# Shifted value tiles made on TensorE, global values fetched in one step, and a newly searched instruction order

## The chip, the cores and the metric

The kernel runs on one core of a Trainium2 chip. The metric is the device time of one execution in microseconds (us). Each time comes with the span between the core's first and last instruction, about 2 us shorter, and with the mean clock that was granted to TensorE (1.00 is full speed). That mean needs care: time for which a trace holds no clock record counts as full speed. The first clock record of the kernel before is at 41.88 us, so a 1.00 earlier than that is no measurement. A run counts as fast when it lies within 1.5% of the fastest run of the same kernel, otherwise as slow, and only fast runs are compared. The five jobs of this study ran on five different chips; the number of the chip of the first comparison is not known, and it is called the first chip. One and the same kernel takes up to 5% longer on one chip than on another (the kernel before took 230.06 and 230.41 us on chips 3 and 2, and 238.42 to 241.22 us in the four other comparisons), so a kernel is always compared with the kernel before in the same job.

## The reference

Four sequences of 768 tokens pass through block-sparse attention (8 heads of 64, blocks of 32 tokens), and the result, with its heads joined, passes through a gated MLP block.

```python
# attention: a query block sees its neighbours, the first and last block,
# and 3 sampled blocks; the first and last query block see everything
mask = np.abs(blk_i - blk_j) <= 1
mask = mask | (blk_i == 0) | (blk_j == 0) | (blk_i == n_blocks - 1) | (blk_j == n_blocks - 1)
for qb in range(n_blocks):
    for kb in sampled_blocks[qb]:
        mask[qb*32:(qb+1)*32, kb*32:(kb+1)*32] = True
...                                    # softmax, then attn @ v
# MLP
h = gelu(x @ w_in); u, v = h[..., :512], h[..., 512:]
v_n = layernorm(v) * g_ln
v_s = np.einsum('ts,bsd->btd', w_sg, v_n) + b_sg[None, :, None]
return x + (u * v_s) @ w_out
```

## The kernel before

The kernel names every operation ("pvR0.2" is the product of probabilities and values over the sampled blocks, batch 0, third tile of 128 tokens). One list, SEQ, fixes the order in which the operations are put on the engines. The semaphore waits are worked out from that order. Each engine is given its operations as one list in that order, so an operation that waits holds up those behind it.

```python
SEQ = """
ldk0.3 ident0 csk0.3:A ident1 warm22:0 ...        # some 1,300 names, :A is the engine, :4 the PSUM bank
"""
```

V of a batch is written to a scratch area in DRAM ("sc") and read back in the layouts that the products need: VG (first and last block), VA (tiles at 0, 128, ...), VS (tiles shifted by 64 tokens) and VR (the sampled blocks, gathered by "ga").

```python
for n in range(2):
    def vg_(e, n=n):
        return e.dma_start(vj[64 * n:64 * n + 64, 0, :, :]..., bass.AP(sc.tensor, sc.offset, ...))
    op("SP", f"vg{b}.{n}", vg_, r=[("scr", bp)], w=[("vjg", n)] + ..., dsem=f"vg{n}", nbytes=66560)
...
op("SP", f"vs{b}", lambda e: e.dma_start(VS[:, :, :, :]..., sc[64:704, :]...), r=[("scr", bp)], w=["VS"], nbytes=665600)
```

The product with the gathered values consists of many short matrix products.

```python
def pvr(pe):
    for h in range(H):
        for ib in range(nbk):
            ins = mm(pe, oap(h, 32 * ib, 32), PR[pr_][0:96, c:c + 32], vslot(rgs[ib])[0:96, h, :])
    return ins
op("PE", f"pvR{b}.{tau}", pvr, r=[okey, ("PR", pr_)] + [("VR", rg) for rg in rgs], mode="32", ...)
```

The softmax here doesn't subtract the row's maximum and nothing guards it: scores larger than these inputs give would overflow.

## Time and profile before

| | before |
|---|---|
| time, median of 3 runs | 241.32 us (240.14 to 242.85) |
| profiled span, TensorE clock | 240.6 us, 0.984 |
| TensorE busy, idle | 206.9 us, 33.7 us |
| "issue" waits of TensorE | 5.9 us, 12 times, at most 0.9 (two of them, 0.7 us, before transposes) |
| DMA moved | 41.51 MB |

TensorE bounds the kernel. What can be saved is its idle time, and most of that lies in the first 37 us. An "issue" wait is a stretch in which TensorE waits for nothing that the profile shows. The views themselves are in the prediction.

### The profile page before, as it was taken

What the parts mean: (1) busy time and instruction counts of PE and PEld (TensorE: products, weight loads), DVE (VectorE), ACT (ScalarE), POOL (GpSimd) and SP (SyncE); (2) the same over time, 40 slices, a digit from 0 to 9 for tenths busy, and PEclk for the clock granted to TensorE, in tenths of its full rate; (3) what the DMA queues carried; (4) which work ended last, traced back from release to release, by engine and by line L of the source; (5) the groups of instructions that cost most, each with busy time, mean ns of one, the idle gap of its engine ahead of it and who ended that gap; (6) DMA issues with size and microseconds to landing.
All of it is one profiled execution on the core that took longest, in us unless ns stands there. A gap on an engine that the chain in (4) does not pass through costs nothing.

```text
span 240.6 us, 8125 instructions
## 1 busy us (share of the span) xinstructions
PE 206.9 (86%) x3282; PEld 164.1 (68%) x3282; DVE 157.0 (65%) x469; ACT 166.9 (69%) x254; POOL 109.3 (45%) x207
## 2 busy tenths in 40 slices
PE   5064538879999989999699999799999999999994
PEld 2053426558887678887488687678886778789672
DVE  2453323645796978894648967648668957577694
ACT  3497926868698946898479666578999677976100
POOL 8215984544384856911547373803472752012000
PEclk9999999988999999999979999999999999999999
DMA  6999999759997795985977975690588123311007
GB/s 191 341 368 282 268 198 228 141 116 235 277 212 178 217 241 75 214 130 183 219 192 169 275 150 185 153 179 9 138 258 208 36 54 119 111 46 44 3 0 262
DMA packets 34457, 41.51 MB, mean 173 GB/s; under 512 B 4804, under 2 KB 27620, under 8 KB 34420
## 3 DMA queue, kind: packets, MB, share of 16 engines
q0 software_dynamic: 14208, 16.20, 35.7%
q1 hardware_dynamic: 20212, 24.80, 34.0%
q8 instruction: 26, 0.43, 0.7%
q14 instruction: 11, 0.09, 0.1%
HBM read 39.72 MB, written 9.55 MB: 205 GB/s over the span
## 4 chain that ended last, share of the span: by engine, by line
PE 78%; ACT 9%; DMA 3%; SPq 3%; issue 3%; another core or an unknown queue 2%; DVE 1%
PE PS L335 68%; PE PS L848 5%; PE PS L521 4%; DMA x_tok<-in_q_dram 3%; ACT PW L707 2%; SPq L480 2%; ACT PR L750 1%; ACT QD L331 1%; ACT PG L724 1%; PE PS L659 1%; ACT w_sgT L331 1%; ACT qn L331 1%; ACT L724 1%; ACT bsg L331 1%
## 5 line engine op out<-in xcount | busy, mean ns | idle before, releaser
L616 POOL DMA_INDIRECT VR<-scr,IDX x44 | 43.2, 982 | 20.5 <-issue 8.3
L637 POOL COPY KR<-KT 128x128 bf16 x88 | 26.0, 328 | 24.7 <-PE PS L335 19.9
L335 PE MATMUL PS<-w_sgT,vh 128*128 128x384 bf16 x192 | 33.5, 326 | 0.0
L633 DVE COPY KR<-KT 128x128 bf16 x176 | 28.3, 226 | 4.1 <-PE PS L335 3.2
L335 PE MATMUL PS<-w_in,xg 128*128 128x512 f32 x96 | 28.3, 422 | 3.1 <-ACT xg L331 2.2
L335 PE MATMUL PS<-w_out,xg 128*128 128x512 f32 x96 | 26.3, 409 | 0.0
L335 PE MATMUL PS<-xg,w_in 128*128 128x384 f32 x128 | 26.2, 351 | 0.0
L916 DVE SCALAR_TENSOR_TENSOR gt<-PS,gcol,bsg 128x384 f32<-128x384 f32 x32 | 19.3, 613 | 10.1 <-PE PS L335 9.3
L335 PEld LDWEIGHTS PS<-w_sgT,vh 128*128 128x128 bf16 x192 | 17.9, 98 | 11.0 <-issue 0.4
L750 ACT ACTIVATE PR<-PS 96x1024 bf16<-96x1024 f32 (+1 forms) x23 | 21.7, 962 | 5.0 <-PE PS L335 2.8
L335 PEld LDWEIGHTS PS<-xg,w_in 128*128 128x128 f32 x128 | 23.1, 194 | 1.7 <-ACT QD L331 0.3
L707 ACT ACTIVATE PW<-PS,b_odd 128x512 bf16<-128x512 f32 (+1 forms) x24 | 15.5, 652 | 9.2 <-PE PS L335 9.2
L335 PEld LDWEIGHTS PS<-w_in,xg 128*128 128x128 f32 x96 | 17.2, 194 | 6.9 <-ACT xg L331 2.7
L874 POOL TENSOR_TENSOR lnt<-lnmv,lnc 128x2 f32<-128x2 f32 x12 | 2.4, 200 | 42.5 <-DVE lnmv L870 41.8
L707 ACT ACTIVATE PW<-PS,b_even 128x512 bf16<-128x512 f32 (+1 forms) x24 | 15.6, 651 | 8.0 <-remote 4.4
L934 DVE TENSOR_TENSOR x_tok<-PS,x_tok 128x512 f32<-128x512 f32 x24 | 16.3, 685 | 5.7 <-PE PS L335 5.5
L869 DVE BATCH_NORM_STATS2 lnst<-vg 128x6 f32<-128x512 f32 x24 | 16.1, 682 | 5.6 <-ACT vg L867 5.6
L829 DVE RECIPROCAL rden<-PS 128x8 f32<-128x8 f32 x24 | 4.9, 205 | 22.7 <-PE PS L335 20.6
L335 PEld LDWEIGHTS PS<-w_out,xg 128*128 128x128 f32 x96 | 17.1, 189 | 3.3
L331 ACT ACTIVATE QD<-PS 64x768 bf16<-64x768 bf16 x18 | 14.4, 803 | 6.3 <-PE PS L335 4.5
L724 ACT ACTIVATE PG<-PS 128x512 bf16<-128x512 f32 x24 | 13.9, 598 | 6.4 <-PE PS L335 6.3
L335 PE MATMUL PS<-VA,PW 128*64 128x65 bf16 x384 | 17.5, 199 | 0.1
(122 smaller groups left out, 438.4 us busy)
## 6 DMA issues: line engine op xcount, KB each, us to landing
out_dram<-x_tok SPq DMA_DIRECT2D x20, 256.0 KB, 2.3
VR<-scr SPq DMA_DIRECT2D x114, 32.5 KB
scr<-vj SPq DMA_DIRECT2D x4, 780.0 KB, 4.7
VS<-scr SPq DMA_DIRECT2D x4, 650.0 KB
kn<-in_v_dram POOLq DMA_DIRECT2D x6, 384.0 KB
kn<-in_k_dram POOLq DMA_DIRECT2D x6, 384.0 KB
qn<-in_q_dram POOLq DMA_DIRECT2D x6, 384.0 KB, 7.3
VA<-scr SPq DMA_DIRECT2D x4, 520.0 KB
```

The lines of the kernel that those rows point to most:

```text
L331: return x.activation(o_, i_, ACT.Copy)
L335: return pe.matmul(o, l, r, start=start, stop=True, skip_group_check=True)
L616: return g.indirect_dma_start(out=vt[0:96, :, :].rearrange("p h e -> p (h e)"), out_offset=None, in_=scr[bp][:, :], in_offset=bass.Indirec ...
L633: ins = x.tensor_copy(KR[:, :, rg, 32 * j:32 * j + 32], KT[:, :, bass.ds(vals["DVE", j, i], 32)])
L637: op("POOL", f"kp{b}.{i}", lambda x, i=i, rg=rg: x.tensor_copy(KR[:, :, rg, 64:96], KT[:, :, bass.ds(vals["POOL", 2, i], 32)]), r=kk + [(" ...
L707: return a.activation(o, i_, ACT.Exp, bias=bias[:, 0:1], scale=SCALE)
L724: op("ACT", f"exG{b}.{tau}", aft=ga, fn=lambda a: a.activation(PG[pg_][:, :], PS[:, uG.slot * 512:uG.slot * 512 + 512], ACT.Exp, scale=SCALE),
L750: return a.activation(PR[pr_][0:96, 0:n], PS[0:96, uR.slot * 512:uR.slot * 512 + n], ACT.Exp, scale=SCALE)
L848: ins = pe.transpose(PS[:, cc:cc + P], x_tok[bp][:, tau, kt * P:kt * P + P], ident_f[:, :])
L869: op("DVE", f"bs{b}.{tau}", lambda x: x.bn_stats(lnst[:, vr, :], vg[vr][:, :]), r=[("vg", vr)], w=[("lnst", vr)], dur=0.6, prio=pr - 300)
L916: op("DVE", f"g1{b}.{c}{dt}", lambda x: x.scalar_tensor_tensor(gt[gr][:, :], PS[:, u.slot * 512:u.slot * 512 + 384], gcol[:, dt:dt + 1], b ...
L934: op("DVE", f"res{b}.{tau}", lambda x: x.tensor_tensor(x_tok[bp][:, tau, :], PS[:, u.slot * 512:u.slot * 512 + 512], x_tok[bp][:, tau, :], ...
```

## The change

The intent was to bring V of batch 0 to the products earlier. The shifted tiles no longer make a DMA trip: TensorE multiplies two neighbouring VA tiles with a shifted identity I3. The two transfers of the global values are issued together and counted as one. Last, the whole order was searched again with measured delays, so that nearly all of SEQ differs. A fourth, small part is in the code that works out the waits: an operation of GpSimd right behind a clear or a padding (names that begin with "ze" or "pa") now waits for it. The core of the diff:

```diff
+    op(("DVE", "POOL"), "i3z", lambda x: x.memset(I3, 0.0), w=["I3"], dur=0.2, prio=-200)
+    op("POOL", "i3", lambda g: g.affine_select(I3, I3, ..., base=64, ...), r=["I3"], w=["I3"], ...)
...
-        for n in range(2):
-            def vg_(e, n=n):
-                return e.dma_start(vj[64 * n:64 * n + 64, 0, :, :]...)
-            op("SP", f"vg{b}.{n}", vg_, ..., dsem=f"vg{n}", nbytes=66560)
+        def vg_(e):
+            return [e.dma_start(vj[64 * n:64 * n + 64, 0, :, :]...) for n in range(2)]
+        op("SP", f"vg{b}.0", vg_, ..., dsem="vg0", nbytes=133120, nd=2)
...
+        if b == 0:
+            for t in range(5):
+                def shf(pe, t=t, u=u):
+                    for c in range(2):
+                        for n in range(2):
+                            ins = mm(pe, PS[:, o:o + 260], I3[:, 128 - 128 * c:256 - 128 * c],
+                                     VA[:, t + c, 4 * n:4 * n + 4, :]..., c == 0)
+            ...                                   # and five evictions she0..4 to VS
+        else:
+            op("SP", f"vs{b}", ...)               # batches 1 to 3 as before
...
-ldk0.3 ident0 csk0.3:A ident1 warm22:0 warm3:N warm10:N warm21:N lnc zeva:P ...
+ident0 ident1 warm19:N bias0 bias1 ldk0.0 lnc i3z:P padk csk0.0:A padv ones iota i3 sbi ...
...                                               # all of SEQ
```

## The prediction

> **What bounds the kernel now.** I read the page first, then the busy table cut into stages, then the waits of TensorE, then the first 45 us of the timeline, and last the chain. The page:
>
> ```profile
> PE 206.9 (86%) x3282; PEld 164.1 (68%) x3282; DVE 157.0 (65%) x469; ACT 166.9 (69%) x254; POOL 109.3 (45%) x207
> ...
> PE   5064538879999989999699999799999999999994
> ...
> ACT  3497926868698946898479666578999677976100
> ...
> DMA  6999999759997795985977975690588123311007
> ```
>
> Each digit is a tenth of busy time in a slice of 6 us. TensorE is nearly full from the eighth slice on, and much emptier before. The idle total is 240.6 - 206.9 = 33.7 us; the question is where it lies. The stage table (stretch; its length; busy time and instruction count of TensorE, weight loads, VectorE, ScalarE, GpSimd; clock; DMA share; GB/s) splits it:
>
> ```profile
> 0.00:22.70 22.70, 8.88 (x55) 5.59 (x55) 8.46 (x33) 14.91 (x22) 9.47 (x24) 1.00 0.90 296
> 22.70:37.20 14.50, 7.09 (x204) 5.59 (x205) 4.75 (x24) 8.90 (x15) 12.94 (x28) 1.00 1.09 235
> 37.20:44.00 6.80, 6.55 (x116) 5.17 (x115) 3.53 (x18) 4.55 (x8) 3.10 (x7) 1.00 0.98 212
> 44.00:60.00 16.00, 13.60 (x344) 10.68 (x343) 8.68 (x24) 11.98 (x16) 7.16 (x12) 0.89 0.79 163
> 60.00:108.00 48.00, 46.55 (x766) 38.07 (x764) 38.72 (x115) 37.65 (x57) 28.24 (x49) 1.00 0.93 194
> 108.00:120.00 12.00, 9.17 (x206) 7.35 (x206) 6.97 (x13) 7.94 (x13) 4.29 (x6) 1.00 0.73 198
> ...
> 145.00:160.00 15.00, 13.29 (x298) 10.53 (x297) 10.30 (x37) 9.64 (x15) 7.80 (x15) 1.00 0.78 185
> ```
>
> Length less TensorE busy: 13.8 us idle up to 22.7 (the loads), 7.4 us to 37.2 (first attention steps), 0.3 to 44, 2.4 to 60, 1.5 to 108, 2.8 to 120, 1.7 between 145 and 160, and 3.2 after 235. These make 33.1; the three stretches not shown hold 0.6. So there are three regimes: a head limited by DMA and then by a wait for V, a long middle limited by TensorE, and an end that no order can shorten much.
>
> What holds the head can be read from TensorE's waits:
>
> ```profile
> PE PS L335 <- DVE VG L332: 2.9, 1, 2.9
> PE PS L335 <- ACT w_sgT L331: 2.6, 1, 2.6
> ```
>
> and from the timeline (start, duration, engine, line, operation, idle time before it and what ended it):
>
> ```profile
> 15.53 0.36 SPq L561 DMA_DIRECT2D scr<-vj  x1
> ...
> 20.27 0.69 SPq L572 DMA_DIRECT2D vj<-scr  x1
> ...
> 21.91 0.52 SPq L582 DMA_DIRECT2D VS<-scr  x1
> ...
> 24.90 0.56 SPq L572 DMA_DIRECT2D vj<-scr  x1
> ...
> 32.13 0.56 DVE L332 COPY VG<-vj 64x260 bf16<-64x260 bf16 x2 [3.49 <-DMA vj<-scr]
> 32.84 0.59 PE L335 MATMUL PS<-VG,PG 128*128 128x130 bf16 x4 [2.90 <-DVE VG L332]
> ```
>
> V of batch 0 is written to a scratch area in DRAM (issued at 15.53, landed by 20.27) and read back in several layouts. The second half of the global values is issued only at 24.90, behind VA, VS and a gather, and its data is usable at 32.13, 7.2 us after issue. The first P x V product starts then. ScalarE, which has already filled the four PW buffers, sits idle from 31.52 to 35.88, and the next score product starts at 37.28.
>
> [...]between 22.7 and 37.2 the share is 1.09, with SyncE and GpSimd transfers in flight together, so a transfer removed or postponed there helps its neighbours. [...]I counted the exp/gelu switches of the old and new ScalarE order, 14 and 14.
>
> **The change part by part.**
>
> *Shifted tiles.* VS of batch 0 no longer comes from DRAM. Removed: one transfer of 650 KB out of a congested stretch; at the 235 GB/s moved there, 665600 / 235000 = 2.8 us of DMA time. Added on TensorE: 5 tiles x 4 matmuls of 260 columns[...]. Added on VectorE: 5 evictions of 128x520 floats; the 128x512 eviction to xg takes 679 ns on it, so about 5 x 0.69 = 3.4 us. Both engines are under half busy from 22.7 to 37.2 (7.09 and 4.75 of 14.5), so most lies beside waiting. Two small I3 set-up instructions go to GpSimd.
>
> *Global values in one step.* Both halves are now issued together, straight after the large VA transfer and ahead of all gathers. With scratch landing near the old 20-22 us, issue comes near 22-23 and landing, at the 4-5 us that a transfer needs in this crowd, at 26-28 instead of 32. Two waits become one in each batch; for batches 1 to 3 I count nothing, since no TensorE wait there names this transfer.
>
> *New order, head.* V is asked for earlier in the load list (transfers 2, 3, 6, 7 of 12). That does not bring scratch forward by much: the loads are 4.7 MB, and DMA moved 190, 340 and 363 GB/s in the stretches to 6, 12 and 16 us, 4.6 MB together, so they fill it until about 16.3 us whatever their order, and the new order also starts both V loads of batch 1 (1.5 MB read) at about 14-16 us, where the old one had only 1 MB of w_in at 16.64. The first scores wait for the last Q eviction on ScalarE. The eighth load was usable at 13.58 before; from there the new ScalarE order has seven casts and evictions of about 0.81 us (5.7), the global keys (1.25), the last Q eviction (0.81) and a copy (0.31): 13.6 + 8.1 = 21.7, against 22.77.
>
> Walking on with durations of this timeline: VA landed by about 26; first shift and eviction to 27.5; five VectorE instructions of 0.4 to 0.7 us until the tile that pvW0.0 needs, about 29.5; first P x V at about 30 against 32.84. Up to the first MLP product (mV0.0) the new order then lists 13 groups of TensorE of 0.5 to 1.1 us each, about 9 us with two of the shifts, hence 40.4 if dense. The old one starts mV0.0 at 42.09, but with one 0.66 us transpose group (xT0.1) less done. **Head gain: 1.7 + 0.7 = 2.4 us, rounded to 2.5**, with the shifts' cost already inside.
>
> *New order, middle.* From 44 to 220 TensorE's idle time is about 9 us. Some 3 us of that are short "issue" gaps that I do not expect order to remove. Of the other 6 (xg 2.2, single waits of 0.5 to 0.9, the Q evictions near 75 and 118) a search with better delays may recover a third to a half, and will add some waits of its own. I take **2 us**.[...]
>
> *End.* Same counts of products, of g1, g2 and residual adds; the order differs in detail. **0 to 0.5 us.**
>
> Sum: 2.5 + 2 + 0.3 = 4.8 us; 241.3 - 4.8 = 236.5. I shade this to **236.3**, since the walk assumes no benefit at all from the 2.8 us of DMA time set free.
>
> **Rivals.**
>
> 1. *The early V loads of batch 1 eat the gain.* They share the 16 engines with the last Q loads and with the scratch write. If shared evenly, scratch lands at about 23 instead of 20.3, and the first P x V at 32 or later. For: DMA share is already 0.90 to 1.09 through the head. Against: a search fed with measured landing delays should have seen it. Time: 239 to 241.
> 2. *The new order removes nearly all V waiting, and TensorE stays dense from 28 us.* The 7.4 us before 37.2 fall to about 2 and the middle gives 4. For: ScalarE is idle 4.4 us in the head only for lack of PW buffers. Against: ScalarE itself is busy 8.73 us of the 10 from 20 to 30. Time: about 232.
> 3. *The saved time is given back in the middle*: batch 1's gathers and loads come no earlier, so an earlier TensorE waits for them. For: DMA share stays 0.93 from 60 to 108. Against: after 44 no TensorE wait names a DMA. Time: about 239.
>
> **Range and chances.** The main estimate lies just at the 2% line (236.5). Rivals 1 and 3 sit above it, rival 2 below, and the middle is uncertain by about 2 us either way. Range 231.5 to 240.5. Faster by over 2%: 0.50; within 2%: 0.45; slower by over 2%: 0.05, since only a disturbed middle of more than 7 us could do that.
>
> **What would show it.** Right: global values copied before 28.5 us; first P x V at 29-31; no ScalarE idle time of 4 us in the head; TensorE idle from 22.7 to 37.2 down from 7.4 to about 4-5;[...] busy time of TensorE about 209 us; the idle time from 44 to 220 near 7 us. Wrong: first scores later than 23 us or scratch read back later than 22 (rival 1); first P x V early but mV0.0 no earlier than 42 (head gain lost to ScalarE or to gathers); a new DMA wait of TensorE after 44 (rival 3).

## The result, and the profile after

| | before | changed |
|---|---|---|
| time, median of 4 runs | 241.22 us | 249.06 us (247.18 to 254.18, the last one slow) |
| profiled span, clock | 240.6 us, 0.984 | 247.3 us, 0.965 |
| TensorE busy, idle | 206.9, 33.7 | 213.2, 34.1 |
| "issue" waits | 5.9 us, 12 times | 11.0 us, 22 times |

The ratio is 1.029, with a 95% interval of 1.020 to 1.039. A ratio here is the mean time of one kernel's fast runs over the mean of the other's of the same rounds, so it is not quite the ratio of the medians. The change made the kernel slower by about 3%.

The page of the changed kernel (busy time; busy tenths of TensorE, its clock and the DMA share in 40 slices of 6.2 us):

```profile
PE 213.2 (86%) x3305; PEld 168.7 (68%) x3305; DVE 160.5 (65%) x474; ACT 166.0 (67%) x253; POOL 112.9 (46%) x210
...
PE   1085577758999998899999989899999797999996
...
PEclk9999999965799999999999999999999998899999
DMA  5999989785793977975999994852056535100107
```

TensorE's idle time is what it was, but its busy time has grown by 6.3 us, and the clock has a dip in the ninth to eleventh slice. The stage table, with the columns of the one in the prediction:

```profile
0.00:22.70 22.70, 8.09 (x60) 6.16 (x60) 11.80 (x40) 14.56 (x22) 13.31 (x33) 1.00 0.96 284
22.70:37.20 14.50, 10.54 (x206) 6.78 (x205) 4.91 (x18) 7.77 (x13) 6.96 (x14) 1.00 1.12 221
37.20:44.00 6.80, 5.50 (x130) 3.99 (x129) 3.99 (x14) 4.36 (x7) 4.02 (x10) 1.00 1.00 211
44.00:60.00 16.00, 10.84 (x254) 7.87 (x255) 4.56 (x25) 10.16 (x13) 8.36 (x14) 0.73 0.77 159
60.00:108.00 48.00, 45.62 (x722) 36.90 (x723) 34.05 (x101) 33.14 (x55) 26.56 (x41) 0.95 0.89 190
```

From 22.7 to 37.2 us the idle time fell from 7.4 to 4.0 us, as hoped, but mainly because the shifts themselves fill 3.1 us of that stretch. From 44 to 60 us it rose from 2.4 to 5.2 us, and the clock there fell from 0.89 to 0.73. The first spatial product of the MLP (mS0) started at 83.3 us instead of 77.3, so 6.0 of the 6.7 us of span are lost by then.

How V came in the head (timeline; start, duration, engine, line, operation, and in brackets the idle time before and what ended it):

```profile
13.60 0.36 SPq L568 DMA_DIRECT2D scr<-vj  x1
14.15 0.97 POOL L507 DMA_DIRECT2D kn<-in_v_dram  x1 [0.47 <-POOL iop L448]
...
20.41 1.27 SPq L578 DMA_DIRECT2D vj<-scr  x2
...
21.73 0.45 SPq L586 DMA_DIRECT2D VA<-scr  x1
...
30.63 0.47 DVE L335 COPY VG<-vj 64x260 bf16<-64x260 bf16 x2 [5.16 <-DMA vj<-scr]
...
31.61 1.04 PE L338 MATMUL PS<-VA,bsg 128*128 128x260 bf16 x4 [2.67 <-DMA VA<-scr]
...
34.43 0.62 PE L338 MATMUL PS<-VG,PG 128*128 128x130 bf16 x4
```

The two halves of the global values are indeed issued together at 20.41, but 10 us pass until they are copied. The first tile of VA, issued at 21.73, comes as late: the shift that needs it ("VA,bsg"; I3 lies in the storage of bsg) waited for it in TensorE's queue until 31.61. A load of batch 1's V (`kn<-in_v_dram`) went out at 14.15, between the scratch write and its read. The first product of probabilities and values starts at 34.43, later than the 32.84 of before.

The long stall lies after 47 us, in the product pvR0.2 (timeline of TensorE alone, other instructions left out):

```profile
47.29 0.31 PE L338 MATMUL PS<-VR,PR 96*32 96x65 bf16 x14
...
48.72 0.19 PE L338 MATMUL PS<-VR,PR 96*32 96x65 bf16 x1 [0.53 <-issue]
...
51.60 0.26 PE L338 MATMUL PS<-VR,PR 96*32 96x65 bf16 x3 [1.20 <-issue]
...
53.02 0.33 PE L338 MATMUL PS<-VR,PR 96*32 96x65 bf16 x7 [0.49 <-issue]
```

These 32 products need about 0.45 us together where nothing disturbs them. Here they took 6 us. They advanced by one to three products and then stood still for about 0.7 us, again and again. They are one operation, which waits for its operands only before its first product, so the operands had been there since 47.29. After it the clock was granted at half speed: from 52 to 66 us the mean was 0.53, against 0.88 before.

The stretch at half clock lay from 51.4 to 65.0 us (mean 0.50) and began 3.8 us after the first of these steps. TensorE was not wholly idle in the steps: it was busy for 2.2 of the 6.3 us from 47.0 to 53.3. That the steps brought on the half clock is my inference from the order in time; no run tests it alone.

The groups of TensorE's instructions by shape show how much of the loss lies in these products (busy time and mean of one; idle time before them). First the kernel before, then the changed one:

```profile
L335 PE MATMUL PS<-VR,PR 96*32 96x65 bf16 x656 | 11.2, 201 | 3.2 <-issue 3.2
```

```profile
L338 PE MATMUL PS<-VR,PR 96*32 96x65 bf16 x656 | 13.1, 204 | 6.7 <-issue 6.7
```

The same 656 products took 14.4 us before and 19.8 after, 5.4 us more.

### The profile page after: what moved, and what is told of

It reads as the page before. It is cut to its first block, busy times and chain, and to the rows that moved or that the text cites.

```text
span 247.3 us, 8185 instructions
## 1 busy us (share of the span) xinstructions
PE 213.2 (86%) x3305; PEld 168.7 (68%) x3305; DVE 160.5 (65%) x474; ACT 166.0 (67%) x253; POOL 112.9 (46%) x210
## 4 chain that ended last, share of the span: by engine, by line
PE 80%; DMA 10%; issue 5%; SPq 2%; DVE 2%; ACT 1%; DVEq 0%
PE PS L338 69%; PE PS L879 5%; DMA vj<-scr 4%; PE PS L528 3%; DMA uT<-in_v_dram 3%; DMA scr<-vj 3%; SPq L487 1%; PE PS L690 1%; DVE VS L335 1%; PE PS L1027 1%; ACT PW L805 0%; ACT vj L334 0%; DVE x_tok L965 0%; SPq L578 0%; DVE gt L947 0%
## 5 line engine op out<-in xcount | busy, mean ns | idle before, releaser
L647 POOL DMA_INDIRECT VR<-scr,IDX x44 | 42.7, 971 | 10.9 <-issue 9.5
L338 PE MATMUL PS<-w_sgT,vh 128*128 128x384 bf16 x192 | 34.4, 326 | 0.0
L664 DVE COPY KR<-KT 128x128 bf16 x176 | 27.1, 220 | 1.1 <-ACT KT L334 0.4
L338 PE MATMUL PS<-w_out,xg 128*128 128x512 f32 x96 | 26.9, 413 | 0.0
L338 PE MATMUL PS<-w_in,xg 128*128 128x512 f32 x96 | 26.4, 408 | 0.0
L338 PE MATMUL PS<-xg,w_in 128*128 128x384 f32 x128 | 24.9, 341 | 0.0
L338 PE MATMUL PS<-VA,PW 128*64 128x65 bf16 x384 | 19.1, 203 | 1.2 <-issue 1.2
L338 PEld LDWEIGHTS PS<-w_out,xg 128*128 128x128 f32 x96 | 17.8, 195 | 3.2
L338 PE MATMUL PS<-VR,PR 96*32 96x65 bf16 x656 | 13.1, 204 | 6.7 <-issue 6.7
L338 PEld LDWEIGHTS PS<-VA,PW 128*64 128x64 bf16 x384 | 15.7, 117 | 3.9 <-issue 2.6
```

Source lines behind the costliest of these rows:

```text
L338: return pe.matmul(o, l, r, start=start, stop=True, skip_group_check=True)
L647: return g.indirect_dma_start(out=vt[0:96, :, :].rearrange("p h e -> p (h e)"), out_offset=None, in_=scr[bp][:, :], in_offset=bass.Indirec ...
L664: ins = x.tensor_copy(KR[:, :, rg, 32 * j:32 * j + 32], KT[:, :, bass.ds(vals["DVE", j, i], 32)])
```

## The experiments

With only the two traces at hand my first theory was that batch 1's scratch write, which the new order issues at 46.05 us just before pvR0.2 instead of at 53.60, fills the DMA engines (their busy share was 0.91 from 47.0 to 53.3 us) and so holds up TensorE's short products. The rivals were the early V loads of batch 1, and the order as such. Two notes on what follows: the profiles of e1, e2, e7 and e9 come from runs that count as slow, so what is read from them is weaker; and the verdicts on record of e0, e6, e7, e9, e11, e15 and e18 are "unclear" (for all but e11 the interval reaches below the limit of 1.02), though all these intervals lie above 1.00.

### First job (chip 3; before: 230.06 us)

**e1_late_scratch** and **e2_late_loads** take the suspected traffic away from the short products.

```diff
+    byname["sc1"].deps.append(byname["mV0.2"])        # e1 and e2
-  ... ldk1.0 ... ldq1.0 ...                            # e2: these two behind kp0.22
```

> The changed kernel with one wait added: the scratch write of batch 1's V waits for the MLP product mV0.2, so it no longer runs beside pvR0.2. Theory S (TensorE's short products starve at 0.7 us steps while that write fills the DMA engines, 47.3 to 53.3 us[...]): the stall shrinks from about 5.5 us to under 2, the half-clock stretch from 13.6 us to under 6, and the time falls from 249 to 240-244 us. Rival O (the loss is in the new order's own dependences and in the shifts' added work): stall and clock stay about as they are or the time stays at 246-250 us.

> As the run with the late scratch write, and two loads of batch 1 (half of K, half of Q) issued only after the last gathers of batch 0. Theory S: if these loads also take part in the stall, a further 0 to 2 us less than the run before it (239-243 us), with no stall over 1 us between 44 and 62 us. Rival O: no gain over the late scratch write alone, or a loss of 1-3 us from K of batch 1 coming late.

Measured: e1 239.4 us in the median, but only one of four runs was fast (235.27 us). e2 took 238.79 us, ratio 1.034 (1.026 to 1.041). In e1 pvR0.2 ran undisturbed (0.45 us), and yet its one fast run took 5.2 us more than the kernel before: "issue" waits came to 5.9 us in all, TensorE waited 4.4 us for VA and 2.9 us for QD. That spoke against the scratch write as the whole cause, but the changed kernel itself had not run on this chip, which turned out to matter.

**e3_before_early_scratch** is the mirror: the kernel before, with its scratch write pulled forward.

```diff
-  ... vc1.0 ...                     # where it was
+  ... vc1.0 rec0.2 ...              # so that sc1 can leave earlier, at 47.80 us
```

> The mirror, in the kernel before: only the VectorE copy that releases the scratch write of batch 1 is moved ahead (before the reciprocal of step 2), so that the write is issued near 48-50 us instead of 53.6, into the short products. Theory S: TensorE's unexplained waits between 46 and 60 us grow from 1.4 to 4 us or more, the clock is low for longer than 3.3 us, and the time rises from 241 to 244-249 us. Rival O: within 1 us of 241, for the copy costs VectorE the same wherever it stands.

Measured: 232.56 us, ratio 1.008 (0.999 to 1.017), "issue" waits of 2.4 us. An early scratch write does not do it alone on this chip. As no kernel stalled in steps on this chip, e3 says nothing for the others.

**e5_old_order** keeps the two new parts and goes back to the order of before.

```diff
-SEQ = (the new order)
+SEQ = (the order before, without vg.1 and vs0, with shf0-4, she0-4, i3z, i3 put in,
+       va0.5 behind padv, exW0.21 and exW0.20 earlier)
```

> The first two parts of the change alone: the order of the kernel before, with batch 0's shifted tiles by TensorE and the global values as one step. Theory S: the two parts are nearly neutral or help a little, first P x V near 29-31 us instead of 32.84, time 238-242 us. Rival O (the added work on TensorE and VectorE is the loss): 244 us or more.

Measured: 231.27 us, ratio 1.004 (0.998 to 1.010). With the old order, and on this chip, the shifted tiles and the single step together cost nothing and gain nothing. Here the loss must sit in the order.

### Second job (chip 15; before: 239.23 us)

**e0_changed** is the changed kernel again. **e6_late_v1** moves the two V loads of batch 1 behind w_in0. **e7_old_head** has the old order up to about 80 us and the new one after it. **e8_new_head** is the opposite. Both mixed kernels allocate PSUM banks anew where the two orders disagree.

```diff
-  sc0 ldv1.0 ... ldv1.1 ... w_in0 ... vc1.1 she3 ... she4
+  sc0 ... w_in0 ldv1.0 ldv1.1 ... she3 ... she4 vc1.1         # e6
+SEQ = old[:"qkR1.5"] + (what is left, in the new order)       # e7
+SEQ = new[:"qkQ1.2"] + (what is left, in the old order)       # e8
```

> The changed kernel itself again, because the chip of the first four runs was some 5% faster than the one of the record (230 against 241 us for the kernel before) and the changed kernel was not measured on it. Both theories: ratio to the kernel before 1.02 to 1.045. If the ratio is near 1.00 the whole loss depended on the chip.

> The changed kernel with batch 1's two V loads moved behind w_in in GpSimd's queue, so that they do not share the DMA engines with the last Q loads and the V scratch of batch 0 (and the VectorE copy that takes them moved after the last shifted tile). Theory V (these loads delay the read-back of V, the first shift product waits for VA at the head of TensorE's queue, and everything behind it is late): wait of TensorE for VA from 3-4 us to under 1, first P x V near 29-31 us instead of 33-34, and 2 to 4 us less than the changed kernel. Rival (the loss is elsewhere in the order, and other transfers simply take the freed place): under 1 us gained.

> Shifted tiles and one-step global values; the order of the kernel before up to the first score products of batch 1, then the new order to the end (PSUM banks given anew where taken). Theory H (the loss lies in the new order's first 80 us): ratio to the kernel before 0.99 to 1.015. Rival M (the loss lies in the later batches' order): ratio 1.02 or more.

> The other half: the new order up to the first score products of batch 1, then the order of the kernel before. Theory H: ratio to the kernel before 1.02 to 1.04, as the changed kernel. Rival M: 0.99 to 1.015.

Measured: e0 246.36 us, ratio 1.028 (1.017 to 1.039); e6 244.61, 1.026 (1.016 to 1.036); e7 245.12, 1.024 (1.017 to 1.032); e8 248.27, 1.038 (1.029 to 1.047).

The loss repeats on another chip, with 10.3 us of "issue" waits. Without the early V loads the first product of probabilities and values starts at 31.5 us instead of 33.1 and mV0.0 at 40.5 instead of 42.5. The fast runs average 242.6 us (two runs) against 245.6 (three), but the intervals overlap. So the early loads cost about 2 us in the head, which shows in the trace, and the effect on the total is not settled. The theory also expected TensorE's wait for VA to fall below 1 us; it went only from 2.6 to 2.2. The mixed kernels put the loss into neither half. Both stalled in short products too, and what their seam costs is not known.

### Third job (chip 2; before: 230.41 us)

Here the control is profiled too. **e13_before** is the kernel before, **e14_old_order_again** is e5, **e15_changed_again** is the changed kernel, and **e9_late_both** joins e6 and e1.

```diff
+    byname["sc1"].deps.append(byname["mV0.2"])        # e9, on top of e6
```

> Control: the kernel before, unchanged, for its trace on the chip of this job. Both theories: ratio 1.00 within 0.7%. Theory supply (short products of TensorE stall in steps of 0.7 us where DMA bursts fall on them): 'issue' waits of TensorE 2 to 5 us, first mS0 product at 74 to 78 us.

> The changed kernel with the order of the kernel before (shifted tiles and single step kept), repeated on another chip. Theory order: ratio 1.000 +- 0.008, 'issue' waits within 2 us of the control's, VG copied 3 us earlier than in the control. Rival (the two new parts cost by themselves and the earlier chip hid it): 1.015 or more.

> The changed kernel, for its trace beside the control's: ratio 1.028 +- 0.008. Theory supply: 'issue' waits of TensorE 5 us or more above the control's, and the half clock in the slices after the long stall; rival (V path): 'issue' waits equal, but TensorE waits 2 to 4 us more for VA and VG in the head.

> The changed kernel with both V loads of batch 1 later and the scratch write of batch 1 held until product mV0.2. If the two costs are separate and add up (2 us of head from the early loads, 4 to 5 us of stall from the scratch write): ratio 1.000 to 1.010, first mS0 near 76 us. If other waits take the place of each (as VA and QD waits did in the run with the late scratch write alone): 1.02 to 1.035, first mS0 79 or later.

Measured: control 229.67 us, 0.998 (0.994 to 1.003); e14 230.97, 1.004 (0.999 to 1.009); e15 234.74, 1.020 (1.014 to 1.026); e9 235.26, 1.019 (1.012 to 1.026).

On this chip the changed kernel still loses 2%, but without the stalls. Its short products took 10.4 us, less than the control's 11.4. Control first, then changed:

```profile
L335 PE MATMUL PS<-VR,PR 96*32 96x65 bf16 x656 | 9.8, 200 | 1.6 <-issue 1.6
```

```profile
L338 PE MATMUL PS<-VR,PR 96*32 96x65 bf16 x656 | 10.0, 199 | 0.4 <-issue 0.4
```

So a loss remains where the stalls don't occur, and the stalls occur on some chips only. Most of the loss of this chip is there when pvG0.2 begins (46.01 us in e15, 43.70 in the control; the spans differ by 3.3). Up to then TensorE waited 4.2 us for VA in e15, and not at all for VA in e14, which has the same two new parts in the old order; this is a comparison of traces and no experiment. On the old order e14 tells more (timeline, columns as above):

```profile
28.44 0.47 DVE L335 COPY VG<-vj 64x260 bf16<-64x260 bf16 x2
...
32.87 0.64 PE L338 MATMUL PS<-VG,PG 128*128 128x130 bf16 x4
```

With the old order the single step brought VG 3.5 us earlier than in the control (31.92). The first product, though, started at 32.87, against 32.57 in the control. TensorE was then held by other things: the shifts in front waited for the score buffer PW.

e9 was meant to recover both losses. Its head did become faster: the first product at 31.4 us and mV0.0 at 40.2 (changed: 33.9 and 43.6). But mS0 started at 76.8 us (in a slow run), hardly before the 77.2 of the changed kernel. GpSimd's timeline shows where the gain went:

```profile
53.06 0.77 POOL L981 DMA_DIRECT2D w_in<-in_moe_w_in_dram  x1
65.05 1.02 POOL L647 DMA_INDIRECT VR<-scr,IDX  x1 [11.22 <-ACT vg L898]
```

GpSimd stood for 11 us in front of a gather that needs the scratch write, now issued at 55.98 and landed at 64.77; the line names ScalarE, but it is this landing that the gather followed. Behind this gather in its queue waited the clearing of QD (2.77 us from 68.20), and so TensorE waited 3.5 us for QD up to 74.5. A wait removed came back as another wait. The run can't tell about the stall, which this chip doesn't have.

### Fourth job (chip 13; before: 239.81 us)

**e16_late_both_free** is e9 with the clearing of QD in front of that gather. **e17_mixed** has the same head, then the old order. **e11_bursts_short** and **e12_bursts_long** are the kernel before with six added writes of 0.8 MB from SBUF to DRAM that nothing waits for.

```diff
-  ... ga1.2 ... zeroq1:P                       # e16, e17
+  ... zeroq1:P ga1.2 ...
+    for n in range(6):                         # e11, e12
+        op("SP", f"bz{n}", lambda e: e.dma_start(dum[:, :], w_in...[:, 0:1560]), ..., nbytes=798720)
+    # released after mO1.1 mO1.5 mV2.0 pvW3.5 pvW3.0 pvG3.3 (e11),
+    #                mV2.3 mU2.13 mU2.00 mU3.13 mU3.01 mS3.01 (e12)
```

> As the run with both V loads and the scratch write late, but GpSimd clears the other half of QD (2.77 us) before the gather that waits for that scratch write. Theory queue (the head gain of that run was lost because GpSimd's queue stood from 53.8 to 65.1 us behind the late scratch and the QD memset came behind it): no TensorE wait for QD near 74 us, first mS0 at 73 to 74 instead of 76.8, ratio 1.000 to 1.010. Rival (the order as such costs, another wait follows at once): first mS0 76 or later, ratio 1.015 or more.

> The same head, then the order of the kernel before from the batch 1 scores on. Theory queue plus theory order (later stages of the new order lose 2 us more than the old ones): ratio 0.985 to 1.005. Rival (the seam between the two orders costs, as it may have in the earlier mixed runs): 1.01 to 1.04 with new TensorE waits between 76 and 110 us.

> The kernel before plus six writes of 0.8 MB that nothing waits for, each released just ahead of short 96x65 products in batches 2 and 3. Theory supply: 'issue' waits of TensorE 3 us or more above the 2 to 5 us of the kernel before, in steps of about 0.7 us, in those stretches; ratio 1.015 to 1.03. Rival (bursts as such do nothing, only late data does): 'issue' waits as before, ratio below 1.01.

> The same six writes released in stretches of 384- and 512-column products. Theory supply: no more 'issue' waits than the kernel before, ratio within 0.6% of 1.00. Rival (a burst costs wherever it falls): as the run with bursts on short products.

Measured: e16 250.78 us, 1.052 (1.046 to 1.058); e17 249.50, 1.045 (1.039 to 1.051); e11 257.46, 1.079 (1.073 to 1.085); e12 243.71 in the median, with few fast runs (241.03 and 241.89 us). One run of the kernel before took 333.97 us in this job, at a clock of 0.609; it counts as slow and is left out.

e16 was a miss, and the most useful one. The scratch write is out of the way until after mV0.2, and pvR0.2 stalls all the same (timeline of TensorE):

```profile
43.80 0.53 PE L338 MATMUL PS<-VR,PR 96*32 96x65 bf16 x15
44.85 0.19 PE L338 MATMUL PS<-VR,PR 96*32 96x65 bf16 x1 [0.52 <-issue]
...
47.22 0.22 PE L338 MATMUL PS<-VR,PR 96*32 96x65 bf16 x2 [1.20 <-issue]
```

That refutes my first theory: the stall doesn't need the scratch write. In e9 the stall was gone because of the chip and not because of the edit, since e15 doesn't have it either. For e1 this is inferred: the changed kernel without the edit never ran on chip 3, but no kernel there stalled in this way. On this chip the stall also delayed mV0.2 to 62.5 us and with it the scratch write that waits for it, and TensorE waited 1.9 us for QD and 3.8 us for VectorE's gt, which stood for the DMA of bsg. That fits the larger ratio of e16, but the changed kernel did not run on this chip. What the reordered queue of GpSimd is worth on a quiet chip was not measured. In e17 TensorE waited 6.0 us for KR up to 84.6, just where the two orders meet: the seam costs, as its rival said, so e17 does not weigh the later stages.

e11 doesn't tell what it was meant to tell. About half of its 18 us are two waits for data: 5.9 us for VA and 3.2 us for VR. Batch 3's VA transfer stood behind an added write in SyncE's queue. A 4.1 us "issue" wait in a short product ended at 161.76, but it began at 157.65, before the added write of 160.92 was issued and after the one before it had landed (156.02). e12's 4.5 us of "issue" waits are no more than the 5.9 of the kernel before on the first chip. So six bursts on long products did not stall TensorE, and whether bursts on short ones do is left open.

### Where the stalls lie

If traffic isn't the trigger, what is? I counted, in every trace, how many TensorE instructions (products and weight loads) had been executed when each "issue" wait began:

| chip | kernel | instructions executed at the "issue" waits |
|---|---|---|
| 2 | before (e13) | 694, 774, 1006, 1199, 3212 |
| 2 | changed (e15) | 692, 1199, 1702, 2710, 3212 |
| first | before | 269, 374, 510-514, 742, 1077-1084, 2128, 3212, 4243, 4411, 5732 |
| 13 | before with bursts (e12) | 374, 507-512, 742, 1074-1080, 2135, 4242, 5734 |
| first | changed | 630-634, 692, 883-904, 1199, 2290-2304, 2620-2653, 3866-3876, 5902-5916 |
| 15 | changed (e0) | 644, 692, 883-902, 1199, 2293-2310, 2616-2651, 3854-3863, 5904-5920 |
| 13 | e16 | 884-902, 1199, 2289-2299, 2619-2657, 3212, 3863-3873, 4475, 5899-5912 |

Nearly all are of two kinds. The first kind lies at 694 + 252n (694, 1199, 1702, 2710, 3212, 4475) on every chip of the table. One count of the page comes near this spacing: in the kernel before, the changed one, e18 and e4 it has 26 packets of 0.43 MB in all on a DMA queue that it calls "instruction", and the 6,564 instructions of TensorE recorded for the kernel before make 252 to a packet, the 6,736 of e18 259 (an estimate from the page). No trace shows that this queue serves TensorE, or that the waits have to do with it.

The second kind appears on the first chip, on 15 and on 13, but not on 2 and 3. In runs of one order it lies at the same places to within some 20 instructions (a few places are missing in some runs), although DMA moved 162 GB/s during the long stall in e16 and 264 in the changed kernel. Two places fit neither kind: 774 in the kernel before on chips 2 and 3, and 1006 in e13.

### Fifth job (chip 0; before: 238.42 us)

**e18_pad** asks whether these places belong to the position in the instruction stream or to the products. It adds 63 one-column products in idle time before the first keys, so that everything later sits 126 instructions further on. **e4_no_shift** takes the shifts out of the new order and reads VS from DRAM again.

```diff
+    def pad(pe, u=u):                                            # e18
+        for n in range(63):
+            ins = pe.matmul(PS[:, u.slot * 512 + n:...+ 1], ident[:, :], ident[:, n:n + 1], start=True, stop=True)
-  ... shf0:2 ... she0 ... i3z:P ... i3 ...                        # e4
+  ... va0.0 vs0 ...
```

> The changed kernel with 63 one-column products (126 TensorE instructions counting the weight loads) added in TensorE's idle time before the first keys arrive, so that every later instruction sits 126 places later in TensorE's stream; nothing else moves. So far 'issue' stalls fell at the same counts of executed TensorE instructions in every trace of this order: near 694 + 252n on all chips (692, 1199, 2710, 3212), and on three of five chips also at 883-904, 2290-2305, 2619-2655, 3855-3875, 5900-5916. Theory position (place in the stream decides): on such a chip the second kind leaves the products that it hit, pvR0.2 is no longer stretched to 6 us, and the time changes by 1% or more either way. Theory group (the products themselves decide): the same products stall, now at 1009-1030, 2416-2431 and so on; time within 1% of the changed kernel's 1.028. On a calm chip: the first kind only, still at 694 + 252n; ratio about 1.02.

> The changed kernel's order with VS of batch 0 read from DRAM again in place of the five shifts. Theory work (of the 3.3 us on a calm chip some 3 us are TensorE work that the order no longer hides): about 2 us less than the changed kernel, ratio 1.010 to 1.015 on a calm chip. Rival (the head ends when V lands, so the shifts cost nothing there): ratio as the changed kernel's, 1.02 or more, with a TensorE wait for VS in place of the shifts. On a chip with the second kind of stall: 40 places earlier in the stream also tests theory position.

Measured: e18 246.34 us, 1.023 (1.016 to 1.031); e4 250.66, 1.052 (1.047 to 1.057). This is a stalling chip too. In e18 the waits of the second kind lie at 1009-1027, 2419-2433, 3976-3986 and 6025-6041, all moved by about 126 places (110 to 129): they stayed with their products. In e4 they lie about 40 places earlier (844-848, 2253-2266, 3808-3817, 5862-5879), again with the same products. The first kind stayed at its counts, as it should: 2711 in e18, and 1197, 1451 and 1703 in e4. pvR0.2 in e18:

```profile
47.08 0.36 PE L338 MATMUL PS<-VR,PR 96*32 96x65 bf16 x14
48.01 0.22 PE L338 MATMUL PS<-VR,PR 96*32 96x65 bf16 x2 [0.56 <-issue]
...
50.15 0.22 PE L338 MATMUL PS<-VR,PR 96*32 96x65 bf16 x2 [1.22 <-issue]
```

The theory of a place in the stream falls for this second kind. Which products are hit does depend on the order, as the rows for the kernel before show.

e4 also corrects a suspicion. I had expected about 2 us less without the shifts. Its fast runs average 250.7 us against 243.9 in e18, and TensorE then waits for the DMA (TensorE's waits in e4: total, times, longest):

```profile
PE PS L337 <- DMA VS<-scr: 5.9, 1, 5.9
```

Inside the new order, with VS issued where e4 has it, the shifts earn more than they cost, so they aren't what makes the order slow.

## Why the prediction was wrong

I had given "slower by over 2%" a chance of 0.05. By its own steps:

- **Head gain of 2.5 us: wrong, it was about zero.** The first scores came at 21.86 us, as predicted (21.7). The next step failed, the read-back of V: "issue comes near 22-23 and landing, at the 4-5 us that a transfer needs in this crowd, at 26-28". Issue came earlier, at 20.41, but VG was copied only at 30.63. "VA landed by about 26" held for the large VA transfer, whose first two shifts ran at 26.52, but not for the small one with VA's first tile, and this was the last of these reads that TensorE waited for, until 31.61. The first product started at 34.43 instead of 30, mV0.0 at 43.87 instead of 40.4. (The walk doesn't add up there: 30 and about 9 make 39.) At about 46 us both kernels were at the same point (the product pvG0.2 began at 46.18 before and 46.24 after). This is rival 1 in part: the early V loads of batch 1 share the DMA engines, and e6 got back 1.6 to 2 us of the head by moving them. But the sign named for it, scratch read back later than 22, didn't come. "A search fed with measured landing delays should have seen it" was no evidence. e14 shows a second error: even with VG at 28.44 the first product did not start earlier, because the shifts stand in front of it in TensorE's queue. In e4, without shifts, it starts 0.5 us after the copy of VG began; in e18, with them, 3.9 us after.
- **Cost of the shifts: the evictions were right, the products were mis-sized.** Five evictions of 0.697 us were measured against the estimate of 0.69. A lone group of four products took 0.93 to 1.04 us, and all five came to 4.7 us, about twice my estimate, which did not come from a trace of these products. Two terms were missing. The first is the time of the last product of a group. In the changed kernel three of these products start 0.12 us apart and the last takes 0.27 (41.58 to 42.09, with 1.00 on record), which makes an estimate of 0.63 us for four in a row; the group at 29.68 in e0 took 0.62 us while the clock on record was 1.00. The second is the clock. The group at 35.71 in e0 took 1.07 us while the clock on record was 0.50 (30.80 to 37.62). The changed kernel has no clock record before 37.72, but its first four groups took about 1 us each and the last one, after it, 0.79. So the 1.00 that the prediction's stage table has for the head is no measurement: e13, the same kernel, has 0.50 on record from 8.20 to 38.91. The shifts also waited 3.5 us in TensorE's queue, 2.7 of them for VA. e4 shows that they were still the better way.
- **Middle gain of 2 us: wrong in sign.** The text says "Some 3 us of that are short 'issue' gaps that I do not expect order to remove". They were 5.9 us over the whole kernel, and I never asked whether a new order could add to them. On this chip it added 5.1 us, and the half clock after the long stall came on top (0.73 instead of 0.89 from 44 to 60 us).
- **Rivals 2 and 3 didn't occur.** No DMA wait of any size took their place after 44 us. The one outcome that I named for "slower", a disturbed middle, was the right kind, but I put 0.05 on it although twelve such gaps stood in the trace before.
- **End: as predicted, nothing.** mS3 starts 6.8 us later than before, and the span is 6.7 us longer.

What is shown: with the old order the two new parts change the time by 0.4% on chips 3 and 2, so on such quiet chips the order carries the loss. The old order with the new parts was not run on a stalling chip. On a quiet chip the changed kernel costs 2.0%, most of it by the first spatial product (77.2 against 74.6 us, of 3.3 us in the span). On stalling chips it is at 1.028 and 1.029 (with e18's padding 1.023), and its products with gathered values take 19 to 21 us (e0: 19.0, e16: 20.0, e18: 20.8) against 14.4 to 14.6 in the kernel before (first chip, e12).

What stays open: why one chip stalls at these products and another does not, and why at just these. The ratios of the two kinds of chips have overlapping intervals, so how much of the end time the stalls make isn't settled either. Nor are "issue" waits all that sets the chips apart: the span of the kernel before is 12.1 us longer on the first chip than on chip 2, and only 2.3 us of that are such waits. Open too is which part of the new order costs the time on a quiet chip; the waits for VA in the head are the first suspect. No experiment beat the kernel before; the best of the new variants, e5 and e14, equals it within half a per cent.

## What to carry to other kernels

Repeat a comparison on more than one chip, with the control profiled beside it: twice a stall seemed cured by an edit, and the other kernels on that chip had no such stall either. Ask of a granted clock whether the trace has a record of it at that time. When an order is searched anew, count the waits that no dependence explains as something that the order can make worse, and look at where each queue will stand still behind a postponed transfer. A part that is worth nothing in one order (the shifts in the old one) can be worth microseconds in another (6.9 us between e4 and e18), so test it in both.
